# Gate and up for four column pairs: product 2 of the two halves of positions made jointly

## The chip, the cores and the metric

One core of a Trainium2 chip runs the whole program in one launch. The metric is the device time in microseconds (us) of one execution; the kernel before took 790.61 us as the median of three runs (789.64 to 792.07). TensorE (PE) multiplies 128x128 tiles with 128x512 tiles into PSUM, with its weight loads listed apart (PEld); VectorE (DVE) and ScalarE (ACT) do the elementwise work; SyncE (SP) issues the loads and GpSimd (POOL) the stores.

## The reference

For x of 2048 positions and 512 features, and F = 1792 hidden columns:

```python
def reference(A_x, A_dft_seq_re, A_dft_seq_im, A_dft_hid_re, A_dft_hid_im, B_x, B_W_gate, B_W_up, B_W_down, gate_w):
    # A: real part of a Fourier transform along features, then positions
    a = einsum("bsd,ed->bse", x, dft_hid_re);  b = einsum("bsd,ed->bse", x, dft_hid_im)
    y = einsum("ts,bse->bte", dft_seq_re, a) - einsum("ts,bse->bte", dft_seq_im, b)
    # B: a gated linear unit with a rectified gate
    h = where(gate > 0, gate, 0) * up            # gate = x @ W_gate, up = x @ W_up
    z = einsum("bsf,fd->bsd", h, W_down)
    # mixed per position
    x = A_x; g = sigmoid((x * gate_w).sum(-1, keepdims=True))
    return g * y + (1 - g) * z
```

(A and B are two inner functions in the reference; B also runs on A_x.)

## The kernel before

**Arithmetic.** Every matrix product in float32 is made of three fp32r matmuls: a value is split in a high part (an ACT cast) and a low part (a DVE subtraction), and PARTS (line 366) names the three pairs, `((1, 0), (0, 1), (0, 0))`, low with high, high with low, high with high. On top of that, products are made in blocks of 2 by 2 by 2 with seven products in place of eight (Winograd's form of Strassen's scheme), whose left and right operands are sums of blocks:

```python
LEFT = {1: ("11",), 2: ("12",), 3: ("12", 6, -1), 4: ("22",), 5: ("21", "22", 1), 6: (5, "11", -1), 7: ("11", "21", -1)}
RIGHT = {1: ("11",), 2: ("21",), 3: ("22",), 4: (6, "21", -1), 5: ("12", "11", -1), 6: ("22", 5, -1), 7: ("22", "12", -1)}
ORDER = (1, 5, 6, 2, 7, 3, 4)
BANK = {1: "x", 2: "x", 5: "m", 3: "m", 6: "y", 7: "y", 4: "t"}
```

PSUM's eight banks are four pairs x, m, y, t (PAIRS). A product accumulates on what its bank holds; a copy by ACT moves a partial result from one bank to the next (product 1 from x to y, product 7 from y to t, negated), and sums kept in SBUF (s5, s6) are added by DVE.

**Gate and up.** A Block(q, w) (lines 493-553) makes gate and up of one column pair c (0 to 6: 128 columns of gate and up in each of two parts of F) for one half q of the positions (two blocks of 512). It runs the seven products in ORDER, 12 matmuls each, 84 in all, each followed by evac (ACT copies, DVE sums u, the rectified product h). Then h_out stores h and four sums of it (hs) to hd in DRAM, the seven right operands for the product with W_down. Weights and w_prep (404-468) load and split the weights of one pair: wr raw, wah and wal high and low of the first factors, ws sums, wb0h, wb0l, wb1h, wb1l their parts, wd.

**Order of the work.** Plan (129-275) records every operation with a key in units of one matmul. PE's order is that of the code; DVE's and ACT's operations are sorted by due times worked out from the keys, SP's loads and POOL's stores by key. 51 units of SBUF are reused in turn, so an early load also has to wait for a free one. In the program's order:

1. Start (962-1020): pairs 0 and 1 together for q = 0, while inputs arrive, in ORDER_S (1, 2, 5, 6, 3, 7, 4); the first block takes products 1 and 2 with high times high first and the low part of the weights (wal) last (line 1009).
2. Pairs 2 to 6, q = 0 and q = 1 each. x of the second half is prepared by x_prep 27 units apart.
3. The transform along features (Spectral, SpectralBlock 596-663), 4 blocks.
4. Tail blocks (1067): pairs 1 and 0 for q = 1.
5. Down(0) and Down(1) (782): h times W_down; its right operands hr are loaded from hd by SP, cast by ACT (ch), subtracted by DVE (cl).
6. The transform along positions: Sequence, Joint(0) (843-932), two Sequences, Joint(1), Last. A Joint makes one product of two halves by the seven products; its right operands jc are the DFT matrix's blocks and sums of them (td). HI, LO = 31, 24 are the units by which the cast jch and the subtraction jcl are ahead of their matmuls, and the raw tile is read 90 ahead (897).

joint_sums (934-940) makes the sums for td: 16 loads (jt), 16 DVE sums and 16 stores of 512 KB, keyed 380 + 160n (1023), that is between 77 and 218 us.

Every operation is recorded through one helper, so that line 126 stands at all rows of the profile; tiles are told apart by name.

Of the kernel before, what the change touches and what calls it, by code (L numbers as in the profile page):

```python
# [14 lines left out]
P = 128  # L15
N = 512
# [262 lines left out]
def kernel(ctx: ExitStack, tc, xP, xG, wgu, wd, cr, ci, wri, gw, out):  # L279
# [94 lines left out]
    def x_load(q, b, ks=slice(0, 2), at=None):  # L374
        k, j = int(b[0]) - 1, int(b[1]) - 1
        (at or load)(piece[q, b][:, ks], xP[2 * q + j, k, :, ks])
# [6 lines left out]
    def x_sum(q, m):  # L383
        if len(RIGHT[m]) > 1:
            a, b = ((piece[q, n] if isinstance(n, str) else X[q, n][2]).all for n in RIGHT[m][:2])
            combine(X[q, m][2].all, a, b, RIGHT[m][2])
# [7 lines left out]
    def x_prep(q, m, key):  # L394
        x_raw(q, m)
        op(key, x_sum, q, m)
        op(key + 7, hi_of, X[q, m])
        op(key + 12, lo_of, X[q, m])
# [75 lines left out]
    def h_out(q, c, h, key):  # L474
        f = [buf(f"hs{n}") for n in range(2)]

        def first():
            e = E()
            e.vector.tensor_add(f[0][:, 0], h[0][:, 0], h[0][:, 1])
            e.vector.tensor_add(f[0][:, 1], h[0][:, 1], h[1][:, 1])  # L480

        def second():
            e = E()
            e.vector.tensor_add(f[1][:, 0], f[0][:, 0], h[1][:, 1])
            e.vector.tensor_add(f[1][:, 1], f[1][:, 0], h[1][:, 0])

        op(key, first)
        op(key + 6, second)
        op(key + 2, lambda: store(hd[q, 0, :, c], h[0][:, 0]))
        for n, t, k in ((1, h[1], 3), (3, f[0], 8), (5, f[1], 14)):  # L490
            op(key + k, lambda n=n, t=t: store(hd[q, n:n + 2, :, c].rearrange("x p n -> p x n"), t.all))

    class Block:


        def __init__(self, q, w, banks=PAIRS):
            self.q, self.w, self.banks = q, w, banks
            self.g = {r: buf("g" + r, (N,)) for r in ("11", "21")}
            self.s = {m: buf(f"s{m}") for m in (5, 6)}
            self.u = {r: buf("u" + r) for r in ("12", "22")}  # L500
            self.h = [buf(f"h{d}") for d in range(2)]
# [8 lines left out]
        def done(self, key):  # L510
            h_out(self.q, self.w.c, self.h, key)
# [6 lines left out]
        def one(self, m, i, k, n, first=0):  # L518
            w, x, ps = self.w.of(m, i, k), X[self.q, m], self.banks[BANK[m]]
            a, b = PARTS[n]  # L520
            mm(ps[i], w[a], x[b][:, k], start=m in FIRST and k == 0 and n == first,
               stop=m in (2, 3, 4, 7) and k == 1 and n == 2 - first)

        def evac(self, m, key):
# [11 lines left out]
            def added(r, ps, s):  # L536
                u, h = self.u[r], self.h[int(r[0]) - 1][:, 1]
                op(key, lambda: e.vector.tensor_add(u.all, ps.all, s.all))
                op(key + 1, lambda: e.vector.scalar_tensor_tensor(h, u[:, 0], 0.0, u[:, 1], op0=OP.max, op1=OP.mult))
# [10 lines left out]
            elif m == 3:  # L550
                added("12", p, self.s[6])
            elif m == 4:
                rectified("21", 0, t, -1.0)

# [59 lines left out]
    class SpectralBlock:  # L614
        def __init__(self, sp, q, ih):
            self.sp, self.q, self.ih = sp, q, ih
            self.s = {m: buf(f"s{m}") for m in (5, 6)}
# [8 lines left out]
        def product(self, m, i):  # L626
            x, w, ps = X[self.q, m], self.sp.w[m], PAIRS[BANK[m]]
# [215 lines left out]
    class Joint:  # L843


        HI, LO = 31, 24
# [40 lines left out]
        def right(self, x, hh, key):  # L887
# [9 lines left out]
            op(key - 90, read)  # L897
# [64 lines left out]
    def x_half(m, k, hi=None):  # L962
        h, l, raw = (t[:, k] for t in X[0, m])
# [8 lines left out]
    for k in halves:  # L972
        op(-99, x_load, 0, "11", k)
        op(-99, ws[0].load, 0, halves[0], k)
    op(-99, ws[1].load, 0, halves[0])
    op(-99, x_load, 0, "21")
    for w in ws:
        op(-99, w.load, 0, halves[1])
    op(-98, x_load, 0, "12")
    for w in ws:  # L980
        op(-98, w.load, 1)
    op(-98, x_load, 0, "22")
    op(-98, lambda: load(gwt[:], gw))
    for k in halves:
        op(-90, x_half, 1, k, plan.vector.tensor_copy)
        op(-90, w_half, ws[0], halves[0], k)
    op(-90, w_half, ws[1], halves[0])
    op(-90, x_half, 2, halves[0])
    op(-90, w_half, ws[0], halves[1])
    op(-90, x_half, 2, halves[1])  # L990
    op(-90, w_half, ws[1], halves[1])
    for n, m in enumerate((5, 6, 3, 7, 4)):
        key = 24 * n + 20
        for f, *a in ((x_sum, 0, m), (hi_of, X[0, m]), (lo_of, X[0, m])):
# [12 lines left out]
    for m in ORDER_S:  # L1007
        for b in start:
            if m in (1, 2) and b is start[0]:
# [8 lines left out]
    for b in start:  # L1018
        b.done(plan.now + 100)
# [3 lines left out]
    for n in range(4):  # L1023
        joint_sums(n // 2, n % 2, 380 + 160 * n)

    sequence = [(2, 0), (2, 1)]
    sequence += [(c, q) for c in range(3, NP) for q in range(2)]
    tail = [(1, 1), (0, 1)]
    spectral = Spectral()

    def blocks(sequence):
        nonlocal w
        for c, q in sequence:
            if w.c != c:
                w = Weights(c)
                if c == 1:
                    w.fetch(plan.now - 140)
                else:
                    w_prep(w, plan.now, 66 if c else 180)
            if c == 2 and q == 0:  # L1040
                for b in ("22", "11", "12", "21"):
                    x_piece(1, b)
                    op(plan.now - 100, x_load, 1, b)
                for n, m in enumerate(ORDER):
                    x_prep(1, m, plan.now - 46 + 27 * n)
            Block(q, w).run()

    blocks(sequence)
# [14 lines left out]

    lefts = [spectrum(f) for f in range(2)]
    for ih in range(2):
        SpectralBlock(spectral, 1, ih)
    blocks(tail)
# [85 lines left out]
```

## Time and profile before

| what | value |
|---|---|
| median of 3 runs | 790.61 us (789.64 to 792.07) |
| the profiled execution | 789.88 us |
| its span (first to last instruction) | 788.1 us |
| granted clock of TensorE, mean | 0.999 |
| ACT's casts of hr for Down, 128x1024 | 42 of 1.049 us |
| DMA moved | 193.84 MB, mean 246 GB/s |

The span is what the trace shows; 1.78 us of the profiled execution lie around it. Rows have the start in us, the duration, the engine, the line, the operation, out<-in, the shapes and a count xN; a bracket at the end is the idle time of that engine just before and what ended it. PE's durations are of one matmul in its pipeline and overlap: the distance of two starts is what a matmul costs in a row of them.

### The profile page before, as it was taken

How to read it: one execution, taken by the hardware profiler on the slowest of the kernel's cores; microseconds unless marked ns; L12 is line 12 of the kernel's file. 1: busy time of each engine (PE TensorE's matmuls, PEld its weight loads, DVE VectorE, ACT ScalarE, POOL GpSimd, SP SyncE). 2: the span in 40 equal slices, each digit the busy share in tenths (PEclk: the TensorE clock that was granted, in tenths of full speed). 3: DMA queues.
4: the chain of work that ended last, by engine and by line, in shares of the span. 5: the costliest groups of instructions: out<-in, count | busy, mean ns of one | idle time of the engine just before them, and what ended most of it. 6: DMA issues, size and time to landing. Idle time of an engine off the chain costs nothing.

```text
span 788.1 us, 9404 instructions
## 1 busy us (share of the span) xinstructions
PE 780.7 (99%) x3435; PEld 644.7 (82%) x3435; DVE 620.4 (79%) x663; ACT 390.4 (50%) x436; POOL 96.1 (12%) x142
## 2 busy tenths in 40 slices
PE   9999999999999999999999999999999999999997
PEld 7888888888888888888888888888888888888885
DVE  7999676667688314978764899967999999989963
ACT  6664333333354335476545464545757365574540
POOL 0011221212122111110000000200020001000200
PEclk9999999999999999999999999999999999999999
DMA  8354775576867975477688798859999889799914
GB/s 324 128 202 166 290 291 214 218 262 242 282 225 233 364 314 184 131 257 293 191 267 315 279 306 311 196 184 294 355 328 270 252 255 188 197 351 330 240 30 81
DMA packets 56574, 193.84 MB, mean 246 GB/s; under 512 B 6608, under 2 KB 6864, under 8 KB 56528
## 3 DMA queue, kind: packets, MB, share of 16 engines
q1 hardware_dynamic: 37552, 124.55, 45.2%
q0 software_dynamic: 18976, 68.69, 29.6%
q8 instruction: 27, 0.44, 0.2%
q14 instruction: 19, 0.16, 0.1%
HBM read 123.99 MB, written 60.83 MB: 235 GB/s over the span
## 4 chain that ended last, share of the span: by engine, by line
PE 97%; ACT 1%; issue 1%; DMA 1%; DVE 0%; SPq 0%; DVEq 0%
PE ps L126 97%; ACT jch L126 1%; DMA wr<-wgu 1%; SPq L126 0%; DVE v L126 0%; DVE z L126 0%; ACT js L126 0%; DVE wal L126 0%; ACT wah L126 0%; ACT ps L126 0%; DVEq L126 0%
## 5 line engine op out<-in xcount | busy, mean ns | idle before, releaser
L126 PE MATMUL ps<-ch,ll 128*128 128x512 f32 x580 | 225.6, 389 | 0.0
L126 PE MATMUL ps<-cl,lh 128*128 128x512 f32 x580 | 225.6, 389 | 0.0
L126 PE MATMUL ps<-ch,lh 128*128 128x512 f32 x580 | 225.6, 389 | 0.0
L126 ACT CAST ch<-r 128x1024 fp32r<-128x1024 f32 x96 | 97.4, 1052 | 72.5 <-DVE r L126 59.9
L126 PEld LDWEIGHTS ps<-ch,lh 128*128 128x128 f32 x580 | 108.9, 188 | 22.7
L126 PEld LDWEIGHTS ps<-ch,ll 128*128 128x128 f32 x580 | 108.9, 188 | 22.7
L126 PEld LDWEIGHTS ps<-cl,lh 128*128 128x128 f32 x580 | 108.9, 188 | 22.4
L126 DVE TENSOR_TENSOR cl<-r,ch 128x1024 fp32r<-128x1024 f32 x96 | 114.6, 1222 | 1.2 <-ACT ch L126 0.6
L126 ACT ACTIVATE ps<-ps 128x1024 f32<-128x1024 f32 (+1 forms) x34 | 32.6, 958 | 87.5 <-PE ps L126 41.0
L126 DVE TENSOR_TENSOR cl<-hr,ch 128x1024 fp32r<-128x1024 f32 (+1 forms) x56 | 59.3, 1088 | 20.4 <-ACT ch L126 18.6
L126 ACT COPY s<-ps 128x1024 f32<-128x1024 f32 x44 | 44.6, 1014 | 52.8 <-PE ps L126 52.8
L126 ACT CAST ch<-hr 128x1024 fp32r<-128x1024 f32 (+1 forms) x56 | 51.3, 942 | 26.7 <-PE ps L126 20.1
L126 DVE TENSOR_TENSOR r<-r,r 128x1024 f32<-128x1024 f32 x48 | 57.2, 1221 | 0.0
L126 POOL DMA_DIRECT2D out<-z x23 | 17.1, 743 | 322.5 <-DVE z L126 322.5
L126 DVE TENSOR_TENSOR u<-ps,s 128x1024 f32<-128x1024 f32 x28 | 34.2, 1221 | 12.4 <-PE ps L126 6.9
L126 PE MATMUL ps<-xh,wb0l 128*128 128x512 f32 x112 | 43.8, 391 | 0.0
L126 PE MATMUL ps<-xl,wb0h 128*128 128x512 f32 x112 | 43.6, 389 | 0.0
L126 PE MATMUL ps<-xh,wb0h 128*128 128x512 f32 x112 | 43.6, 389 | 0.0
L126 PE MATMUL ps<-xh,wb1h 128*128 128x512 f32 x112 | 43.6, 389 | 0.0
L126 PE MATMUL ps<-vh,xh 128*128 128x512 f32 x112 | 43.6, 389 | 0.0
L126 PE MATMUL ps<-vh,xl 128*128 128x512 f32 x112 | 43.6, 389 | 0.0
L126 PE MATMUL ps<-xh,wb1l 128*128 128x512 f32 x112 | 43.6, 389 | 0.0
(126 smaller groups left out, 1311.2 us busy)
## 6 DMA issues: line engine op xcount, KB each, us to landing
hr<-hd SPq DMA_DIRECT2D x42, 512.0 KB, 4.5
r<-cr SPq DMA_DIRECT2D x32, 512.0 KB, 5.7
r<-ci SPq DMA_DIRECT2D x32, 512.0 KB, 5.8
hd<-hs POOLq DMA_DIRECT2D x28, 512.0 KB, 5.2
out<-z POOLq DMA_DIRECT2D x23, 512.0 KB, 6.4
td<-jt POOLq DMA_DIRECT2D x16, 512.0 KB, 3.9
ad<-a POOLq DMA_DIRECT2D x16, 512.0 KB, 3.9
l<-ad SPq DMA_DIRECT2D x16, 512.0 KB, 7.2
```

The lines of the kernel that those rows point to most:

```text
L126: getattr(getattr(nc, self.engine), self.name)(*map(ap, self.a), **{k: ap(x) for k, x in self.k.items()})
```

## The change

Product 2 has the left block 12 and the right block 21, and its result goes to the output block 11 alone. For one column pair it is a product of 2 (gate, up) x 2 (blocks of 128 features) by 2 (features) x 2 (halves of positions), 8 products of one tile each, 24 matmuls for both halves. For pairs 3 to 6 the change makes it by the same seven-product scheme, 7 x 3 = 21 matmuls.

- **JointX** prepares the seven right operands jx1 to jx7 once, from the "21" pieces of x of both halves. **JointW** makes per pair four sums of weight parts of 128 columns (jws, on DVE), their high parts (jw, a cast on ACT) and low parts (DVE). Its products write bank x, one of its two banks as Y and the other as M; partial results are kept in jv and jo.
- **Joined** is a Block without product 2. With q = 0 it runs 5, 1, (joint 5, 1), 6, (joint 6), first half of 3, (joint 3, 7), 7, second half of 3, (joint 2, 4), 4; with q = 1 it runs 1, 5, 6, first half of 3, 7, second half of 3, 4. The block 11 of the output is then the sum of product 1 and jo, and a relu and product as for the others. Product 7's copy to t is made in two operations of 512.
- **Start:** both first blocks, not only the first, take products 1 and 2 with wal last. Their h is stored without the sums; **h_late** reads it again during the spectral blocks and makes the sums then.
- x's pieces "21" are loaded again ahead of the spectral blocks and split again, which frees their units in between; x_prep of the second half is 24 units apart.
- joint_sums has keys 1300 + 120n (about 295 to 393 us). Joint's HI, LO are 26, 20, and its read is 82 ahead. The two tail blocks are written out.

Over the program this makes 96 matmuls of product 2 fewer and 84 new ones.

What moves is seen in the engines' orders. The names are tiles with the number of the recording. First DVE at the boundary from pair 2 to pair 3; u are the sums of products 7 and 3 of the last block of pair 2, h its rectified results, ws and wb0l the weights of pair 3. Before:

```order
L126 TENSOR_TENSOR h_693<-g_675,ps 128x512
L126 TENSOR_TENSOR ws_700<-wr_619,wr_631 128x512
L126 TENSOR_TENSOR wb0l<-ws_685,wb0h 128x1024
L126 TENSOR_TENSOR u_713<-ps,s_636 128x1024
L126 TENSOR_TENSOR ws_700<-wr_619,ws_685 128x512
L126 TENSOR_TENSOR u_723<-ps,s_659 128x1024
```

And with the change:

```order
L126 TENSOR_TENSOR wb0l<-ws_677,wb0h 128x1024
L126 TENSOR_TENSOR jws<-wr_626 128x128
L126 TENSOR_TENSOR u_710<-ps,s_648 128x1024
L126 TENSOR_TENSOR jws<-jws,wr_626 128x128
L126 TENSOR_TENSOR jws<-wr_626 128x128
L126 TENSOR_TENSOR jws<-wr_626,jws 128x128
L126 TENSOR_TENSOR h_723<-g_681,ps 128x512
L126 TENSOR_TENSOR ws_730<-wr_626,wr_641 128x512
L126 TENSOR_TENSOR jw<-jws,jw 128x512
L126 TENSOR_TENSOR u_741<-ps,s_665 128x1024
```

Between the two sums u stood one subtraction for weights; now there stand six operations, and wb0l stands ahead of the first.

Second, ACT in the second half (q = 1) of pair 3. The first row copies product 1 from bank x to y, the two s are products 5 and 6, g is the gate of block 11, ACTIVATE ps is product 7's copy; wah, wb0h and jw belong to pair 4. Before:

```order
L126 COPY ps<-ps 128x1024
L126 COPY s_923<-ps 128x1024
L126 COPY s_941<-ps 128x1024
L126 ACTIVATE g_949<-ps 128x512
L126 CAST wah<-wr_909 128x1024
L126 ACTIVATE ps<-ps 128x1024
L126 CAST wb0h<-ws_975 128x1024
```

And with the change:

```order
L126 COPY ps<-ps 128x1024
L126 COPY s_957<-ps 128x1024
L126 CAST wah<-wr_921 128x1024
L126 CAST jw<-jws 128x512
L126 COPY s_983<-ps 128x1024
L126 CAST wb0h<-ws_973 128x1024
L126 ACTIVATE ps<-ps 128x512 x2
L126 CAST wb1h<-ws_1006 128x1024
```

The casts of wah and jw now stand ahead of the copy of product 6, and the cast of wb0h between that copy and product 7's.

Third, ACT in Joint(0); jch are the casts of the right operands, js the copies of products 5 and 6, ACTIVATE ps product 1's copy. Before:

```order
L126 CAST jch<-jc 128x1024
L126 CAST jlh<-js_4058 128x1024
L126 CAST jch<-jc 128x1024 x5
L126 ACTIVATE ps<-ps 128x512
L126 CAST jch<-jc 128x1024 x4
L126 COPY js<-ps 128x512 x2
L126 CAST jwh<-jr 128x1024
```

And with the change:

```order
L126 CAST jlh<-js_4184 128x1024
L126 CAST jlh<-js_4200 128x1024
L126 CAST jch<-jc 128x1024 x5
L126 ACTIVATE ps<-ps 128x512
L126 CAST jch<-jc 128x1024 x4
L126 COPY js<-ps 128x512
L126 CAST jch<-jc 128x1024
L126 COPY js<-ps 128x512
L126 CAST jwh<-jr 128x1024
```

The first copy js comes after nine casts jch instead of ten, and one cast stands between the two copies.

The diff, cut to its core:

```diff
+    def h_late(q, c, key):
+        h = [buf(f"hk{d}") for d in range(2)]
+        for i, n in enumerate((0, 3)):
+            op(key - 20 + i, lambda i=i, n=n: load(h[0][:, i], hd[q, n, :, c]))
+        op(key - 18, lambda: load(h[1].all, h_forms(q, c, 1)))
+        h_sums(q, c, h, key)
...
+    class Joined(Block):
+        def run(self, joint=None):
+            slots = {(1, 1): (5, 1), (6, 1): (6,), (3, 0): (3, 7), (3, 1): (2, 4)}
+            for m, i in (*((m, i) for m in ((1, 5) if self.q else (5, 1)) for i in range(2)), (6, 0), (6, 1), (3, 0), (7, 0), (7, 1), (3, 1), (4, 0), (4, 1)):
+                pe(6, self.product, m, i)
+                if i:
+                    self.evac(m, plan.now)
+                for y in slots.get((m, i), ()) if joint else ():
+                    joint.step(y)
+        def done(self, key, joint):
+            self.added("11", self.s[1] if self.q == 0 else self.banks["x"], joint.o[self.q], plan.now)
+            super().done(key)
...
+    class JointW:
+        def __init__(self, w, x, key):
...
+            op(key - 30, lambda: combine(raw[:, 0], s[:, 1, 0, 1], s[:, 1, 1, 1], 1))
+            op(key - 30, lambda: combine(raw[:, 2], s[:, 1, 0, 0], s[:, 1, 0, 1], -1))
+            op(key - 29, lambda: combine(raw[:, 1], raw[:, 0], s[:, 1, 0, 0], -1))
+            op(key - 28, lambda: combine(raw[:, 3], s[:, 1, 1, 0], raw[:, 1], -1))
+            op(key - 24, lambda: E().scalar.copy(self.t[:, 0], raw.all))
+            op(key - 20, lambda: E().vector.tensor_sub(self.t[:, 1], raw.all, f32(self.t[:, 0])))
+        def step(self, y):
+            pe(3, self.product, y)
+            self.evac(y, plan.now)
...
-        HI, LO = 31, 24
+        HI, LO = 26, 20
...
-            op(key - 90, read)
+            op(key - 82, read)
...
-            if m in (1, 2) and b is start[0]:
+            if m in (1, 2):
...
-        b.done(plan.now + 100)
+        b.done(plan.now + 8, False)
...
-        joint_sums(n // 2, n % 2, 380 + 160 * n)
+        joint_sums(n // 2, n % 2, 1300 + 120 * n)
...
-                    x_prep(1, m, plan.now - 46 + 27 * n)
+                x_prep(1, m, plan.now - 46 + 24 * n)
+            jx = JointX(plan.now + 70)
...
+            pair = [Joined(q, w) for q in range(2)]
+            joint = JointW(w, jx, plan.now)
+            for q, b in enumerate(pair):
+                b.run(None if q else joint)
+                b.done(plan.now + 8, joint)
+    for q in range(2):
+        x_piece(q, "21")
+        op(plan.now - 150 + 60 * q, x_load(q, "21"))
+        x_prep(q, 2, plan.now - 100 + 100 * q)
...
+    for c in range(2):
+        h_late(0, c, plan.now + 30 * c)
```

159 lines of the change are left out of this document (112 added, 47 removed).

## The prediction

> **What bounds the kernel now.** I read three views of the profile of before, in this order: the page's shares, the waits of PE, and the chain of waits.
>
> ```profile
> PE 780.7 (99%) x3435; PEld 644.7 (82%) x3435; DVE 620.4 (79%) x663; ACT 390.4 (50%) x436; POOL 96.1 (12%) x142
> PE 97%; ACT 1%; issue 1%; DMA 1%; DVE 0%; SPq 0%; DVEq 0%
> ```
>
> The first line gives the busy time of each engine, the second the engines' shares of the chain that ended last. PE is busy for 99% of the span and is 97% of that chain, so the end of the program is the end of a row of matmuls. A matmul less shortens it by that matmul, and nothing else shortens it except a wait of PE. Those are few (columns: us in total, times, longest):
>
> ```profile
> PE ps L126 <- DVE warm L126: 1.2, 1, 1.2
> PE ps L126 <- ACT js L126: 0.5, 2, 0.3
> PE ps L126 <- DVE wal L126: 0.4, 1, 0.4
> ```
>
> The first belongs to the warm-up, which the change leaves. The other two, 0.9 us together, are in places that it does touch.
>
> ```profile
> 8.16 542.15 PE ps L126 x2387
> ```
>
> This is a link of the chain: start, length, number. From 8.16 us on PE runs 2387 matmuls with no wait long enough to break the link, 542.15 / 2387 = 0.227 us each.
>
> The profiled execution took 789.88 us, of which 788.1 are the span and 1.78 lie around it; the median of the runs is 790.61. I make the sum as a difference and take it from both.
>
> **The matmuls.** Per column pair from 3 to 6, product 2 takes 2 halves x 12 = 24 matmuls now and 7 x 3 = 21 then. Over four pairs that is 12 fewer, and the new ones have the same shape (128x128 by 128x512).
>
> ```profile
> 67.28 0.39 PE L126 MATMUL ps<-xh,wb0l 128*128 128x512 f32 x1
> 70.00 0.39 PE L126 MATMUL ps<-xh,wb0l 128*128 128x512 f32 x1
> ```
>
> These two rows stand 12 matmuls apart in a stretch without waits: 70.00 - 67.28 = 2.72 us, the value of 12. (The 0.39 is one matmul's length in the pipeline, not its spacing.) Term one: **-2.72 us**.
>
> **The start.** Both first blocks now take their products 1 and 2 with the high parts first and wal, the low part of the weights, last.
>
> ```profile
> 6.76 0.62 ACT L126 CAST wah<-wr 128x512 fp32r<-128x512 f32 x1 [0.70 <-DMA wr<-wgu]
> 7.14 0.61 PE L126 MATMUL ps<-xh,wal 128*128 128x512 f32 x2
> 7.42 0.69 DVE L126 TENSOR_TENSOR wal<-wr,wah 128x512 fp32r<-128x512 f32 x1 [0.62 <-ACT wah L126]
> 8.16 0.50 PE L126 MATMUL ps<-xh,wal 128*128 128x512 f32 x1 [0.41 <-DVE wal L126]
> 11.02 1.29 DVE L126 TENSOR_TENSOR wal<-wr,wah 128x512 fp32r<-128x512 f32 x2
> 11.95 0.40 PE L126 MATMUL ps<-xh,wal 128*128 128x512 f32 x1
> 16.66 0.47 PE L126 MATMUL ps<-xh,wb0l 128*128 128x512 f32 x1
> 19.51 0.50 PE L126 MATMUL ps<-xh,wb0l 128*128 128x512 f32 x1
> ```
>
> The second block's first matmul came at 8.16; behind the two at 7.14 it could have come at 7.14 + 2 x 0.227 = 7.59, so 0.57 us are lost to wal, which ends at 7.42 + 0.69 = 8.11. In the new order the first four matmuls need only wah, there from 6.76 + 0.62 = 7.38, and wal at the fifth, at 7.59 + 4 x 0.227 = 8.50, after 8.11. So the 0.57 goes. What is late next is DVE: the next wal, the first of the pair at 11.02, ends at 11.71, was used at 11.95 and would now be wanted at 11.38; its order up to there is unchanged, so some 0.37 are given back and 0.2 stay. The rows at 16.66 and 19.51 are 0.1 longer than the usual 0.39: two short waits for wb0l. Ahead of that tile DVE's new order has one sum of weights less (0.6 us), which covers the 0.2, so both go: 0.2 + 0.1 + 0.1, I take **-0.45**. Ends: 0 (all is given back) and -0.8 (0.57 and the two waits).
>
> **The joint product of the DFT.** Casts and subtractions of jch and jcl come five and four matmuls nearer to their use (31, 24 to 26, 20).
>
> ```profile
> 551.81 3.88 ACT L126 CAST jch<-jc 128x1024 fp32r<-128x1024 f32 x4
> 555.58 0.39 PE L126 MATMUL ps<-jch,jlh 128*128 128x512 f32 x1
> 555.59 1.05 ACT L126 COPY js<-ps 128x512 f32<-128x512 f32 x2
> 556.21 0.50 PE L126 MATMUL ps<-jch,jll 128*128 128x512 f32 x1 [0.25 <-ACT js L126]
> 556.55 0.40 PE L126 MATMUL ps<-jcl,jlh 128*128 128x512 f32 x1
> ```
>
> ACT makes four casts in a row and only then copies the banks that PE needs. PE's spacing is 0.63 and 0.34 instead of 0.227 twice: 0.40 + 0.11 = 0.51 us, at each of the two Joints. In the changed order the first copy stands one cast (about 1 us) earlier and the second behind one cast more; the first wait goes whole, some of the second may stay. For both Joints **-0.8**; ends 0 and -1.0.
>
> **A new wait ahead of pair 3.** The first joined block starts with product 5 instead of 1. Product 5 writes bank m, which the block before frees with its last sum (u, of product 3); it is needed 12 matmuls earlier than before, and DVE has four new subtractions of 128 columns (jws) ahead of it.
>
> ```profile
> 44.16 0.39 PE L126 MATMUL ps<-xh,wal 128*128 128x512 f32 x1
> 77.16 1.00 ACT L126 ACTIVATE ps<-ps 128x1024 f32<-128x1024 f32 x1
> 78.43 1.22 DVE L126 TENSOR_TENSOR u<-ps,s 128x1024 f32<-128x1024 f32 x1
> 79.56 0.68 DVE L126 TENSOR_TENSOR ws<-wr,ws 128x512 f32<-128x512 f32 x1
> 80.16 1.22 DVE L126 TENSOR_TENSOR u<-ps,s 128x1024 f32<-128x1024 f32 x1
> L126 DVE TENSOR_TENSOR wal<-wr,wah 128x256 fp32r<-128x256 f32 x2 | 0.8, 422 | 0.0
> L126 DVE TENSOR_TENSOR hs<-hs,h 128x512 f32<-128x512 f32 x28 | 19.1, 689 | 0.3
> ```
>
> PE reaches pair 3 at 44.16 + 168 x 0.227 = 82.25. On DVE the first u waits for ACT's copy of product 7 (the row at 77.16, which can start 0.1 sooner): from about 78.05, its pitch is 79.56 - 78.43 = 1.13, three ops of 512 columns follow at 80.16 - 79.56 = 0.60, the second u takes 1.22. The width of 128 is in no row: 422 ns at 256 and 689 at 512 give 1.04 ns a column, so an estimate of 0.29 us, 0.2 in pitch. The sum is 78.05 + 1.13 + 3 x 0.2 + 3 x 0.60 + 1.22 = 82.80, and some 0.1 until PE sees it: **+0.7** on PE. What is queued behind that u on DVE (its relu, then the low parts of pair 3) has 12 matmuls to spare. Ends: 0 (the first u ready earlier) and 1.5 (DVE begins at 78.43 and takes the jws at full length).
>
> **ACT in the pairs.** In a joined second half only six matmuls of product 3 stand between 6 and 7, which share bank y, where the old order had 12; in the first half the same holds between 1 and 6.
>
> ```profile
> 68.42 0.39 PE L126 MATMUL ps<-xh,wb0h 128*128 128x512 f32 x1
> 68.84 1.01 ACT L126 COPY s<-ps 128x1024 f32<-128x1024 f32 x1 [0.62 <-PE ps L126]
> 246.97 1.23 DVE L126 TENSOR_TENSOR vl<-v,vh 128x1024 fp32r<-128x1024 f32 x1 [1.73 <-DMA hd<-h]
> ```
>
> An ACT that is idle begins its copy 68.84 - 68.42 = 0.42 after the last matmul began, and takes 1.01; with 0.05 until PE restarts that is 1.48 against 7 x 0.227 = 1.59 until the next write. So the eight places fit by 0.1 us each as long as ACT is free. In the second half it is so narrowly: between the ends of products 5 and 6 lie 2.72 us, and ACT has product 5's copy, the cast of wah (1.05, as the cast ch further below) and that of jw (0.62, as the row at 6.76) to do, 2.68. The other new place is the row at 246.97: DVE's tile for the spectral products had 1.7 us of waiting to give, and new sums come ahead of it. I take **+0.2** for both; ends 0 and 2.0.
>
> **What is covered.** The preparation of jx and jw, the later sums for h, and the shift of the sums for the DFT (16 loads and 16 stores of 512 KB from 77-218 us to some 295-393 us) are on DVE, ACT, SP and POOL. DVE is busy 79% and ACT 50% of the span, and PE hides them except at the places above; the queues are a rival below.
>
> **The sum**: -2.72 - 0.45 - 0.8 + 0.7 + 0.2 = -3.07. Of the profiled execution that makes 789.88 - 3.07 = 786.8, of the median 790.61 - 3.07 = **787.5 us**. About 0.3%, 2.4 us, is what a measurement of this kernel can tell from no change, so faster means below 788.2.
>
> **The rivals.**
>
> *ACT is late in each second half.* If the cast of jw only begins when product 6 ends, its 0.62 less the margin of 0.1 are left on PE, 0.5 at four places, +2.0: **789.5**. For it speaks how full ACT is there; against it that the casts are due early and that ACT is half idle else.
>
> *The waits stay.* Where DVE sets the pace, an earlier PE only waits elsewhere: the start gives 0, the Joints 0, the boundary costs 1.5, ACT 0.2, and 790.61 - 2.72 + 1.7 = **789.6**. For it speaks the short wait at 16.66; against it that the waits view names none of PE's after 8.16 but js.
>
> *A matmul is worth less than its spacing.* If half of the spacing were left behind by each, the 12 would bring 1.36, and the time would be **788.9**; 2387 matmuls at 0.227 speak against it. The Trainium skill (TensorE: Matmul & The Clock Gate, section Back-to-back issue gap) gives a sustained spacing of about 131 ns for 512 columns; by that figure term one would be an estimated 1.57 us. The trace's 227 ns differs, and the measurement decides.
>
> *Slower: Down's loads come late.* The moved loads and stores meet the reloads of h for Down.
>
> ```profile
> 295.00:366.00 71.00, 71.00 (x314) 58.72 (x313) 55.39 (x61) 40.89 (x47) 8.28 (x12) 1.00 0.64 223
> 546.00:565.00 19.00, 18.75 (x83) 15.19 (x83) 18.64 (x18) 16.77 (x20) 0.84 (x1) 1.00 1.02 350
> 321.89 27.74 SPq L126 DMA_DIRECT2D hr<-hd  x11
> 348.86 0.39 PE L126 MATMUL ps<-xh,wd 128*128 128x512 f32 x1
> hr<-hd SPq DMA_DIRECT2D x42, 512.0 KB, 4.5
> td<-jt POOLq DMA_DIRECT2D x16, 512.0 KB, 3.9
> L126 DVE TENSOR_TENSOR cl<-hr,ch 128x1024 fp32r<-128x1024 f32 x42 | 51.0, 1222 | 19.4 <-ACT ch L126 17.6 <-PE ps L126 1.2 <-issue 0.3
> L126 ACT CAST ch<-hr 128x1024 fp32r<-128x1024 f32 x42 | 43.7, 1049 | 19.5 <-PE ps L126 13.5 <-DMA hr<-hd 4.7 <-DVE cl L126 1.3
> SPq L126 <- DVE cl L126: 55.8, 26, 8.8
> ```
>
> The last two numbers of a window are the DMA share and GB/s. From 295 to 366 the engines moved 223 GB/s, at full share (546 to 565) 350. The 32 transfers are 16.8 MB over 98 us, 171 GB/s more: 394, or 44 too many, which leaves 3.1 MB, 9 us of work, standing at 366; as the windows are uneven I take 12. The first hr is issued at 321.89 and Down starts after 348.86: 27 us, less 4.5 to land, 1.05 to cast and 1.22 to subtract leaves 20.2. The price begins there. SP stands up to 8.8 us for a free buffer; if it stands so at two of the new loads ahead of hr, the delay is 12 + 17.6 = 29.6, and 9.4 us reach PE: **796.9**. Against it: one such stand alone (20.8) is just absorbed. In a sentence by itself, the Trainium skill (DMA: Bandwidth & Descriptors, section Issuing engines are not separate DMA queues) says that transfers run on the same 16 engines whichever engine issued them, so that SP's loads and POOL's stores would not evade each other.
>
> **How the numbers follow.** Forecast 0.59, late ACT 0.15, waits stay 0.15, matmuls worth less 0.02, slower 0.09. The low end takes the better bounds: 790.61 - 2.72 - 0.8 - 1.0 = 786.1, so 786.0. The high end is the dearest of the rivals that are not slower, 789.6, and 0.8 for the spread of the medians: 790.4. Only the late loads lie outside. Below 788.2 are the forecast's cases unless two of its losses are larger, 0.58; above 793.0 the late loads, 0.09; the rest is 0.33.
>
> **What would show it.** Right: 12 matmuls fewer, no wait for wal at 8 us, at most one short wait for js at each Joint, and one wait of PE for a u of 0.5 to 1 us at 82 us. Wrong: waits of PE for ACT's s at the sixth matmuls of the pairs; a wait for ch or cl soon after 346 us, with a DMA share near 1 ahead of it (late loads); or PE reaching 234 us no earlier than before (the pairs give back what they save).

## The result, and the profile after

The changed kernel took 788.81 us, the median of 10 runs (787.85 to 790.92), against 790.39 us for ten runs of the kernel before. The ratio is 0.998, with a 95% interval of 0.9972 to 0.9988: 1.6 us less, between 0.9 and 2.2. The forecast was 787.5, with a range of 786.0 to 790.4. The profiled execution took 789.17 us, with a span of 787.3; that is 0.7 less than the profiled one of before.

The page of the changed kernel, busy time and chain:

```profile
PE 778.7 (99%) x3423; PEld 641.5 (81%) x3423; DVE 652.6 (83%) x716; ACT 403.2 (51%) x465; POOL 96.9 (12%) x144
PE 92%; issue 2%; DVE 2%; DMA 1%; ACT 1%; POOL 0%; SPq 0%; DVEq 0%; ACTq 0%; POOLq 0%
```

There are twelve matmuls less and 2.0 us less of busy PE, but PE's share of the chain has fallen from 97% to 92%: the chain now leaves PE in places where it did not before. PE's waits, in the same columns as before:

```profile
PE ps L126 <- DVE warm L126: 1.2, 1, 1.2
PE ps L126 <- DVE vl L126: 1.1, 1, 1.1
PE ps L126 <- ACT wah L126: 0.5, 1, 0.5
PE ps L126 <- DVE u L126: 0.5, 1, 0.5
```

The waits for wal and js are gone from the list, and three others stand in it. A wait in this list is only the part in which PE was idle; what it costs is the distance of two starts less the usual 0.227 us. Added up over the starts of all matmuls that gives, for the two profiled executions:

| place | before | after | difference | forecast |
|---|---|---|---|---|
| 12 matmuls | | | -2.72 | -2.72 |
| start: pair 2 begins at | 44.16 | 44.07 | -0.1 | -0.45 |
| boundary to pair 3 | 0 | 0.73 | +0.7 | +0.7 |
| second halves of pairs 3 to 6 | 0 | 0.28 | +0.3 | +0.2, with the next |
| features' transform, 248 us | 0 | 1.35 | +1.35 | |
| two Joints | 1.03 | 0.66 | -0.4 | -0.8 |
| sum | | | -0.8 | -3.1 |

The sum is that of the two spans, 787.3 - 788.1 = -0.8; what the table leaves out (small spacings between these places, the time behind the last matmul) is about 0.1 each and cancels. So the table says where the expected time went, in these two executions. The medians differ by 1.6 and not by 0.8; which of the places is cheaper in the other executions wasn't recorded. PE reached the features' transform at 233.07 us, 1.65 earlier than before (234.72): the pairs give back the two rows of 0.7 and 0.3 and keep the rest. Four places in rows, first the start:

```profile
7.69 0.62 ACT L126 CAST wah<-wr 128x512 fp32r<-128x512 f32 x1 [1.54 <-DMA wr<-wgu]
8.36 0.51 PE L126 MATMUL ps<-xh,wah 128*128 128x512 f32 x1 [0.51 <-ACT wah L126]
```

ACT waits for the load of weights wr, which landed 0.93 us later than before (7.69 against 6.76); PE waits for the high part instead of the low one. Then the boundary to pair 3:

```profile
77.95 1.23 DVE L126 TENSOR_TENSOR u<-ps,s 128x1024 f32<-128x1024 f32 x1 [1.05 <-ACT ps L126]
79.49 0.28 DVE L126 TENSOR_TENSOR jws<-wr,jws 128x128 f32<-128x128 f32 x1
81.50 1.22 DVE L126 TENSOR_TENSOR u<-ps,s 128x1024 f32<-128x1024 f32 x1
82.77 0.50 PE L126 MATMUL ps<-xh,wb0l 128*128 128x512 f32 x1 [0.46 <-DVE u L126]
```

The first u begins at 77.95, six operations follow, the second u ends at 82.72 and PE starts 0.05 later. The 128-column subtraction took 0.28. Third, the features' transform, on POOL, DVE and PE:

```profile
237.10 0.72 POOL L126 DMA_DIRECT2D hd<-h  x1 [15.22 <-DVE h L126]
238.84 0.55 POOL L126 DMA_DIRECT2D hd<-h  x1 [1.02 <-DVE h L126]
hd<-h POOLq DMA_DIRECT2D x1, 512.0 KB, 6.7
hd<-h POOLq DMA_DIRECT2D x1, 256.0 KB, 5.6
241.12 1.22 DVE L126 TENSOR_TENSOR xl<-x,xh 128x1024 fp32r<-128x1024 f32 x1
243.88 1.23 DVE L126 TENSOR_TENSOR vs<-v,vs 128x1024 f32<-128x1024 f32 x1 [1.54 <-DMA hd<-h]
246.86 1.22 DVE L126 TENSOR_TENSOR vl<-vs,vh 128x1024 fp32r<-128x1024 f32 x1
248.14 0.50 PE L126 MATMUL ps<-vl,xh 128*128 128x512 f32 x1 [1.08 <-DVE vl L126]
```

The third and fourth row give the size of the two stores above them and the time until they landed. h_out stores block 11 in one transfer of 256 KB and the blocks 21 and 22 in one of 512 KB, so the first store is that of 21 and 22, and it landed at 237.10 + 6.7 = 243.8. The sum vs, for the left operand of product 3, waits 1.54 us for just this landing. It reads nothing of h: it needs a unit of SBUF that h still holds. Three of the gate's reductions and vl come behind it, and PE stands. In the kernel before the same two operations, and the same two stores, read:

```profile
227.81 0.58 POOL L126 DMA_DIRECT2D hd<-h  x1 [4.98 <-DVE h L126]
239.13 1.22 DVE L126 TENSOR_TENSOR vs<-v,vs 128x1024 f32<-128x1024 f32 x1
239.52 0.71 POOL L126 DMA_DIRECT2D hd<-h  x1 [11.13 <-DVE h L126]
241.47 1.23 DVE L126 TENSOR_TENSOR vl<-vs,vh 128x1024 fp32r<-128x1024 f32 x1
```

There vs waited for nothing, and vl was ready almost 6 us before its use. Block 11 was stored at 227.81, now at 238.84, 11 us later. The blocks 21 and 22 were stored at 239.52, 2.4 us later than now, and the tile that waited for that landing was the last vl (the row at 246.97 in the prediction), which was ready at 248.20, 3 us before its use. Last, Joint(0) on ACT and PE:

```profile
551.28 3.91 ACT L126 CAST jch<-jc 128x1024 fp32r<-128x1024 f32 x4
555.09 0.57 ACT L126 COPY js<-ps 128x512 f32<-128x512 f32 x1
555.57 1.04 ACT L126 CAST jch<-jc 128x1024 fp32r<-128x1024 f32 x1
555.71 0.50 PE L126 MATMUL ps<-jch,jll 128*128 128x512 f32 x1
556.05 0.39 PE L126 MATMUL ps<-jcl,jlh 128*128 128x512 f32 x1
```

PE, which arrives about 0.3 earlier than before, still starts when the first copy ends: its spacing there is 0.45 and 0.34 instead of 0.63 and 0.34. As before, four casts stand in a row right ahead of that copy; they begin 0.53 earlier (551.28 against 551.81).

### The profile page after: what moved, and what is told of

Read it like the earlier page. It is cut to its first block, busy times and chain, and to the rows that moved or that the text cites. A ratio compares the mean times of both kernels' runs of the same rounds, so it can differ in the third digit from the quotient of the medians.

```text
span 787.3 us, 9523 instructions
## 1 busy us (share of the span) xinstructions
PE 778.7 (99%) x3423; PEld 641.5 (81%) x3423; DVE 652.6 (83%) x716; ACT 403.2 (51%) x465; POOL 96.9 (12%) x144
## 4 chain that ended last, share of the span: by engine, by line
PE 92%; issue 2%; DVE 2%; DMA 1%; ACT 1%; POOL 0%; SPq 0%; DVEq 0%; ACTq 0%; POOLq 0%
PE ps L126 92%; DMA hd<-h 1%; DVE u L126 1%; DMA wr<-wgu 1%; POOL hd L126 0%; DVE h L126 0%; DVE gx L126 0%; ACT jch L126 0%; SPq L126 0%; DVE v L126 0%; DVE z L126 0%; DVE vl L126 0%; ACT ps L126 0%; ACT js L126 0%; ACT wah L126 0%
## 5 line engine op out<-in xcount | busy, mean ns | idle before, releaser
L126 ACT COPY s<-ps 128x1024 f32<-128x1024 f32 x48 | 48.7, 1014 | 68.1 <-PE ps L126 64.1
L126 PE MATMUL ps<-vl,xh 128*128 128x512 f32 x112 | 43.7, 390 | 1.1 <-DVE vl L126 1.1
L126 PE MATMUL ps<-xl,wb1h 128*128 128x512 f32 x112 | 43.6, 389 | 0.0
```

The lines of the kernel that those rows point to most:

```text
L126: getattr(getattr(nc, self.engine), self.name)(*map(ap, self.a), **{k: ap(x) for k, x in self.k.items()})
```

## The experiments

Each kernel was timed beside the kernel before; the ratios are to that one, with 95% intervals of 0.0008 to 0.0017 to each side. The changed kernel's own ratio is 0.998. Every edit is made to the changed kernel.

**1. The gate's reductions later.** Do they make the wait for vl?

```diff
-        gate(t, plan.now + 30 + 50 * t)
+        gate(t, plan.now + 90 + 50 * t)
```

> The changed kernel, with the gate's reductions (gx on DVE) keyed 60 units (13.6 us) later, so that none stands ahead of the low parts vl for the third product of the features' transform. Theory: PE's wait of 1.24 us for vl at 248 us, with 0.11 behind it, is made by three gx operations of 0.61 us pitch behind a sum that itself waited 1.54 us for a store of h to land; without them vl ends near 246.2, before PE wants it at 246.9, the wait goes whole and nothing else is late next: 1.3 us less than the changed kernel, 787.5 us, 0.9963 of the kernel before. Rival: the landing of the store sets the time, gx only fills it, and the next vl or the sums a come late instead: no gain, 788.8, with a wait of about 1 us under another name between 246 and 260 us.

It took 789.21 us, ratio 0.9986 (0.9978 to 0.9995). The wait for vl was gone, but the time was not less. The move gave the units of SBUF and DVE another order later on, and in the Sequence PE waited for cl:

```profile
495.94 0.50 PE L126 MATMUL ps<-cl,lh 128*128 128x512 f32 x1 [0.48 <-DVE cl L126]
```

With what follows that is 0.75, and at 227 us another 0.37. Pair 2 also began 0.5 later in that execution (44.59). And vs began at 235.40 without a wait for a unit, so the run doesn't tell the reductions from the unit. It shows that the wait can be taken away, not what it is worth.

**2. jws and jw later.** All six operations of JointW on weights get keys 20 higher:

```diff
-            op(key - 30, lambda: combine(raw[:, 0], s[:, 1, 0, 1], s[:, 1, 1, 1], 1))
+            op(key + 20 - 30, lambda: combine(raw[:, 0], s[:, 1, 0, 1], s[:, 1, 1, 1], 1))
```

> The changed kernel, with the preparation of the four weight sums (jws and jw) keyed 20 units (4.5 us) later, so that on DVE only two subtractions of weights stand between the two sums u at the boundary to pair 3. Theory: the wait for u at 82.8 us (0.62 and 0.11) is DVE's queue, and the second u ends near 81.6 before PE arrives at 82.1: that wait goes, and so do the four of 0.07 at the casts of jw ahead of product 6's copy in the second halves: 0.7 to 1.0 less than the changed kernel, 787.9 us. Rival: the wait moves to the low part wb1l or to jw, which are now behind the u, within the first joined block: 0.3 less at most, 788.5.

It took 788.36 us, ratio 0.9976 (0.9967 to 0.9984): less than the changed kernel, but inside both intervals. In the trace PE runs over the boundary without a stop:

```profile
82.28 0.39 PE L126 MATMUL ps<-xh,wd 128*128 128x512 f32 x1
82.51 0.39 PE L126 MATMUL ps<-xh,wb0l 128*128 128x512 f32 x1
```

The 0.73 were DVE's queue, as forecast. The small waits of the second halves stayed at 0.06 to 0.07 each, although no cast of jw stands ahead of product 6's copy any more, so these don't come from it; that part of the expectation was wrong. This execution also shows the wait at 248 us in a dearer form, in the last section.

**3. No joint product.** Pairs 3 to 6 made by plain blocks:

```diff
-            pair = [Joined(q, w) for q in range(2)]
-            joint = JointW(w, jx, plan.now)
-            for q, b in enumerate(pair):
-                b.run(None if q else joint)
-                b.done(plan.now + 8, joint)
+            for q in range(2):
+                Block(q, w).run()
```

> The changed kernel, with pairs 3 to 6 made by plain blocks (product 2 for each half, 12 matmuls more over the program; no jx, jw) and everything else as changed. Theory: 12 matmuls cost their spacing, 2.72 us, and the waits that came with the joint products (0.73 for u at the boundary, 0.28 at the copies of product 6) go: 1.7 above the changed kernel, 790.5 us. If the wait for vl belongs to the end of the last joined pair it goes too: 789.2. Rival: a matmul is worth half its spacing here: 0.35 above the changed kernel, 789.2, with the spacing between neighbouring matmuls of product 2 below 0.2 us in the trace.

It took 790.0 us, ratio 0.9996 (0.9987 to 1.0004). PE had no wait at the boundary, none in the second halves and none for vl (0.1 at 251 us; 0.33 at 270 us is new), so by the trace it is the second of the two cases expected, though the median lies 0.8 above its value. The profiled execution fits it: 789.17 + 2.72 - 0.73 - 0.28 - 1.35 = 789.5, and it took 789.58. So the waits of the table that are new in the changed kernel come with the joint product, and what else the change does is worth about nothing beside the Joints' 0.4. Between neighbours of product 2 the spacing is 0.227.

**4. The old order at the start.**

```diff
-            if m in (1, 2):
+            if m in (1, 2) and b is start[0]:
```

> The changed kernel, with the old order of the second first block (products 1 and 2 with the low part of the weights first), all else as changed. Theory: the profile of the changed kernel showed no gain at the start only because its load of weights landed 0.9 us later in that execution; for the same landing the old order waits 0.6 us longer, of which DVE's row gives some back: 0.4 us above the changed kernel, 789.2. Rival: after 11 us DVE sets the pace of the start whatever PE's order is, and nothing is lost: 788.8.

It took 788.80 us, ratio 0.9985 (0.9976 to 0.9994): that of the changed kernel. In its profiled execution the load came late and the old order did wait longer:

```profile
9.29 0.50 PE L126 MATMUL ps<-xh,wal 128*128 128x512 f32 x1 [1.53 <-DVE wal L126]
```

Pair 2 began at 44.78 us here. In the eight traces with the new order and as late a load (landing at 7.5 to 8.0) it began between 44.07 and 44.59, so with a late load the new order was 0.2 to 0.7 earlier than this one execution of the old. With an early load (6.4 to 6.9) it began between 43.97 and 44.43, in experiments 2, 3 and 7, and before, with the old order, at 44.16. There the new order only moves the wait: PE had none at 8 us and stood at 11 us for the next wah, here in experiment 7:

```profile
11.17 0.73 PE L126 MATMUL ps<-xh,wah 128*128 128x512 f32 x2 [0.60 <-ACT wah L126]
```

In the twelfth trace, of experiment 6, it began at 46.05: the first loads landed 1 us later, and the clock came to its full speed only at 9.45 us, in the others by 7.3. In the median the new order is worth nothing that can be seen.

**5. The features' operands nearer together.** This puts vs ahead of the sums of h and vl ahead of the gate, and leaves the later order as it is.

```diff
-        spectral.prep(m, plan.now - 44 + 16 * n if n < 3 else plan.now - 30 + 12 * n)
+        spectral.prep(m, plan.now - 44 + 16 * n if n < 3 else plan.now - 30 + 10 * n)
```

> The changed kernel, with the operands of the features' transform prepared 10 units apart from product 2 on and not 12, so that on DVE the sum vs for product 3 stands ahead of the four sums of h, and its low part vl ahead of the gate's reductions; the gate's keys stay. Theory: PE's wait for vl at 248 us (1.35 with what follows, and more in runs where the store of h lands later or the clock sinks behind it) is that place in DVE's queue; it goes, and nothing later is reordered: 1.3 less than the changed kernel, 787.5 us, with less spread between the runs. The kernel with the gate moved lost the same wait and gained nothing in the median because its later order made a wait of 0.75 for cl at 496 us and one at 227. Rival: the wait for vl is in few runs only, so that the median does not move: 788.6 to 788.9; or vs itself now holds DVE up until the store lands: a wait of PE for vl or xl of about 1 us as before, 788.8.

It took 789.87 us, ratio 0.9996 (0.9987 to 1.0004), slower than the changed kernel. vs was done at 238.3, but another tile now stood for the unit of h, ACT's copy of product 6:

```profile
244.90 1.01 ACT L126 COPY s<-ps 128x1024 f32<-128x1024 f32 x1 [1.16 <-DMA hd<-h]
245.97 0.50 PE L126 MATMUL ps<-vh,xl 128*128 128x512 f32 x1 [1.53 <-ACT s L126]
```

This ended the theory that the place in DVE's queue makes the wait. The store that s waited for is that of block 11, issued at 239.17 and landed at 244.8, not the one that vs waits for in the changed kernel. Whoever takes a unit of h waits until its store has landed.

**6. Three edits at once**: experiments 2 and 5, and HI, LO = 24, 18.

> The changed kernel with three edits: the features' operands 10 units apart, jws and jw 20 units later, and HI, LO of the Joints 24, 18 (first copy js after eight casts). Theory: the waits add up, 1.35 for vl, 0.73 for u and 0.28 in the second halves, 0.66 at the Joints: 3.0 less than the changed kernel, 785.8 us, 0.994 of the kernel before. Rival: DVE and ACT are full at these places and the waits come back under other names, half of it at most: 787.3.

It took 788.75 us, ratio 0.9988 (0.998 to 0.9997). No wait was left at the boundary or at the Joints, but ACT's s cost 2.04 us at 247, as in 5. The profiled execution was the slowest of the twelve (791.94), so how much of the 2.9 that the median lacks is due to s isn't shown.

**7. The sums for the DFT back in the pairs.**

```diff
-        joint_sums(n // 2, n % 2, 1300 + 120 * n)
+        joint_sums(n // 2, n % 2, 380 + 160 * n)
```

> The changed kernel, with the sums for td back at their old keys (16 loads, sums and stores between 77 and 218 us and not 295 to 393). Theory: where they are PE never waits for them, neither here nor there; the reloads hr have 20 us in hand and lose 3.5 us in landing; the time is that of the changed kernel within 0.5: 788.8. Rival one (late loads): the moved transfers cost PE something in Down, and undoing them gains 0.5 or more: 788.3 or less. Rival two: with the joint products DVE has no room for 16 sums of 1.22 us in the pairs, and PE waits there for u, jo or wb0l: 789.5 or more.

It took 792.63 us, ratio 1.0027 (1.0017 to 1.0037): 3.8 above the changed kernel. The number falls under rival two, but the path that it named isn't there: no wait for u or jo was added in the pairs; in the profiled execution (791.05 us) the loss stands at the features' transform:

```profile
245.05 0.50 PE L126 MATMUL ps<-vh,xl 128*128 128x512 f32 x1 [0.67 <-ACT s L126]
250.13 0.50 PE L126 MATMUL ps<-vl,xh 128*128 128x512 f32 x1 [1.83 <-DVE vl L126]
```

That is 3.05 us with what follows, against 1.35. So moving the sums away belongs to the change: without it more than its gain is lost. The rest of the median's loss isn't in this execution, and its place stays open.

**8. The Joints as before.** HI, LO = 31, 24 and the read at 90.

> The changed kernel, with HI, LO of the Joints and the read back at 31, 24 and 90. Theory: the wait for js at each Joint is 0.51 again and not 0.33, 0.37 for both: 789.2 us, and the rows at 555 and 705 us are as in the kernel before. Rival: the wait at the Joints is set by what PE brings with it, not by the place of the copy, and stays at 0.33: 788.8.

It took 788.87 us, ratio 0.9983 (0.9975 to 0.9992); 0.4 us can't be told in the median. In the trace the rows of before are back, 0.64 and 0.34 between starts at both Joints, 0.37 more in all:

```profile
555.71 0.50 PE L126 MATMUL ps<-jch,jll 128*128 128x512 f32 x1 [0.26 <-ACT js L126]
556.05 0.40 PE L126 MATMUL ps<-jcl,jlh 128*128 128x512 f32 x1
```

**9. Block 11 of a second half summed early.**

```diff
                 if i:
                     self.evac(m, plan.now)
+                    if m == 1 and self.q:
+                        self.added("11", self.banks["x"], self.jo, plan.now)
...
-            self.added("11", self.s[1] if self.q == 0 else self.banks["x"], joint.o[self.q], plan.now)
+            if not self.q:
+                self.added("11", self.s[1], joint.o[0], plan.now)
...
             for q, b in enumerate(pair):
+                b.jo = joint.o[q]
                 b.run(None if q else joint)
```

> The changed kernel, with the output block 11 of a joined second half (q = 1) summed right after product 1 and not after product 4, so that it is no longer the last of the block's results and its store to hd is issued some 9 us earlier; all later orders on DVE stay. Theory: the tile that PE waits for at 246 to 250 us (vl, or ACT's s in the kernel with the features' operands nearer) has to take a unit of SBUF from h, which is free only when h's store has landed, at 243.9; the change made that store the last of the block. With the sum early PE has no wait over 0.2 us there: 1.3 less than the changed kernel, 787.5 us, and less spread. Rival: the unit comes free with the other part of h (21 and 22), whose store is as late as before: the wait stays at 0.8 to 1.7, 788.8.

It took 788.93 us, ratio 0.9978 (0.9969 to 0.9987), the changed kernel's within the intervals; the runs lay between 788.34 and 789.38, a spread of 1.0 against 3.1. vs no longer waited and the wait for vl was gone, but the next tile in want of a unit waited for the store of the sums hs:

```profile
246.27 1.23 DVE L126 TENSOR_TENSOR vl<-v,vh 128x1024 fp32r<-128x1024 f32 x1 [0.94 <-DMA hd<-hs]
250.94 0.50 PE L126 MATMUL ps<-vh,xl 128*128 128x512 f32 x1 [0.69 <-ACT ps L126]
```

It reaches PE as 0.95 us through DVE's sums and ACT's copy, and at 227 us PE lost 0.31 where it lost 0.07 before. So the late sum of block 11 did cause the wait of vs, but not by the path that was expected. Block 11 was stored at 225.63, 13 us earlier; the store of 21 and 22, for which vs had waited, was issued at 237.24 and landed at 243.4, about when it does in the changed kernel, but vs began at 240.52, before that landing: it got another unit. Units are so short there that a later tile then waited for the next store, and the rival's number came.

**10. Early sum, late jws, and HI, LO = 24, 18 together.**

> The kernel with the early sum of block 11, and jws and jw 20 units later, and HI, LO of the Joints 24, 18. Theory: 1.35 for vl, 0.73 for u, 0.2 in the second halves and 0.66 at the Joints go: 2.9 less than the changed kernel, 785.9 us, 0.994 of the kernel before. Rival: the start, which is ruled by the landing of the first loads, and one place that is late next keep a third of it: 786.9.

It took 787.28 us (786.63 to 787.52), ratio 0.9958 (0.9945 to 0.997): by medians and by ratios faster than the kernel before by 3.1 and 3.3 us, and than the changed kernel by 1.5 and 1.7 (with the intervals, between 0.6 and 2.9). PE's waits:

```profile
PE ps L126 <- DVE warm L126: 1.2, 1, 1.2
```

Only the warm-up is left in the list; shorter than the list shows are 0.31 at 226 us and 0.06 at three places. The expected 785.9 was 1.4 too low; the 0.95 of experiment 9 wasn't in its profiled execution (span 784.9, 786.63 us), which was the fastest of its runs.

**11. The sums for the DFT in half the time.**

```diff
-        joint_sums(n // 2, n % 2, 1300 + 120 * n)
+        joint_sums(n // 2, n % 2, 1360 + 60 * n)
```

> The changed kernel, with the sums for td made in less time: 16 loads, sums and stores keyed 1360 + 60n and not 1300 + 120n, so that they share the time with the first reloads hr for Down. Theory of the prediction: DMA carries no more than 350 GB/s, the loads hr come late by the backlog, and PE waits for ch or cl between 346 and 400 us by 3 us or more: 792 us or above. Rival: the changed kernel's windows show 401 to 416 GB/s at 335 to 395 us, so there is room left, SP issues hr in time, and PE does not wait there: 788.8 within 0.4.

It took 797.82 us, ratio 1.009 (1.0073 to 1.0107). This is the rival of late loads. ACT waits for hr, and PE for ACT and DVE:

```profile
370.06 1.04 ACT L126 CAST ch<-hr 128x1024 fp32r<-128x1024 f32 x1 [5.54 <-DMA hr<-hd]
371.16 0.50 PE L126 MATMUL ps<-ch,ll 128*128 128x512 f32 x1 [1.42 <-ACT ch L126]
372.42 0.50 PE L126 MATMUL ps<-cl,lh 128*128 128x512 f32 x1 [0.76 <-DVE cl L126]
```

From 371 to 397 us PE lost 7.8 us. A load hr took up to 18.9 us to land, in the changed kernel up to 13.9 and before up to 8.4. So the mechanism exists; the changed kernel's spacing of 120 units stays clear of it, as no wait for ch or cl stands in its list.

**12. No joint product, and HI, LO = 24, 18**: the counterpart of 10.

> The changed kernel with pairs 3 to 6 made by plain blocks (12 matmuls more, no jx, jw) and HI, LO of the Joints 24, 18: what is left of the waits of the kernel with the early sum (787.28 us) on both sides of the joint product. Theory: the 12 matmuls cost their spacing of 2.72, less the 0.3 to 0.5 that the joint pairs still wait at their copies: 787.28 + 2.3 = 789.6 us, with PE waiting nowhere over 0.3 us after 12 us. Rival: a matmul is worth half its spacing: 787.28 + 1.36 - 0.4 = 788.2 us.

It took 789.35 us, ratio 0.9989 (0.998 to 0.9998), with no wait of PE but the warm-up's in the list (0.33 at 270 us is below what it shows). Against experiment 10 that is 0.9989 - 0.9958 = 0.0031 of 790.4, or 2.4 us, with the intervals between 1.2 and 3.7. The profiled spans say the same, 787.3 - 784.9 = 2.4: on ground without the other waits the twelve matmuls bring their 2.72 less about 0.3, which is what PE's small waits differ by. Against experiment 3, which differs by HI, LO alone, it is 0.0007 or 0.6 us, inside the intervals, and in the traces the 0.68 that the Joints cost there and not here.

## Why the prediction was right, and where it was off

The direction and the range held; half of the forecast gain came. The range is a weak test: its upper end is 790.4, which is what the kernel before itself measured over ten runs. The 788.81 is also above the 788.2 below which the prediction called the result faster, in the case that it gave a chance of 0.33. And the number is nearest to that of a rival that is wrong, the matmul worth half its spacing with 788.9: there it is coincidence, as the rows below show. Step by step:

- **The matmuls: right.** The term of 2.72 for 12 matmuls agrees with the balance of the two traces and with the 2.4 us between experiments 12 and 10. The rival of a matmul worth half its spacing is out: it gave 1.36 - 0.4 there, and would leave 1.36 of the balance without a place.
- **The boundary: right.** 0.73 measured against 0.7, by the path that was named; experiment 2 takes it away by DVE's order alone.
- **The start: wrong.** The step took the landing of one execution's load as given. It lay between 6.4 and 8.0 us in fourteen traces. With a late one the new order waits for wah where the old one waited for wal, and with an early one it waits at 11 us instead, where the step gave back 0.37 of 0.57 and 0.4 to 0.9 were lost. Median gain: none that experiment 4 could see, where 0.45 were forecast.
- **The Joints: half.** PE does wait for that copy, but the step took it to come one cast, about 1 us, earlier, and 0.37 came for 0.8. Nine casts stand ahead of it and not ten, but the four in a row between product 1's copy and js, on which the step rests, stayed four. So the copy came only 0.5 us earlier, and as PE came 0.3 earlier too, 0.2 of the wait went. The prediction said "the first wait goes whole"; with three casts in that row (HI, LO = 24, 18, experiments 6 and 10) it does.
- **The features' transform: mis-sized, and with the wrong cause.** The prediction saw that vl's slack of 1.7 us would shrink and booked 0.2 with ACT's small waits, where 1.63 came. It looked for the cost in DVE's queue. The cost was a unit: vs was given one that held the blocks 21 and 22 of h, whose store was still on its way. That store isn't late, it is issued 2.4 us earlier than before. What is late is block 11: the joint product makes it the last result of a block, stored 11 us later. Experiment 9 shows that this is the cause (with the sum early vs gets another unit), and 5 that units stay short (another tile waits, for the store of block 11). That the late sum works by keeping its own tiles' units in use is argued, not shown.
- **ACT in the second halves: about right.** 0.07 at each of four places, not 0.5. Moving jw's cast left them, and in experiment 2 ACT stood idle ahead of product 6's copy, so no cast delays it; that the copy itself uses up the margin of 0.1 is likely, but not shown.
- **Late loads: rightly a rival, rightly kept small.** Its price was built on 350 GB/s as the most that DMA moves, and that was wrong:

```profile
335.00:355.00 20.00, 20.00 (x90) 16.57 (x89) 19.93 (x23) 13.01 (x16) 4.88 (x8) 1.00 1.01 401
355.00:375.00 20.00, 20.00 (x90) 16.57 (x89) 20.00 (x23) 11.97 (x13) 2.74 (x4) 1.00 1.03 412
375.00:395.00 20.00, 20.00 (x89) 16.54 (x89) 17.36 (x18) 11.56 (x14) 2.15 (x4) 1.00 1.03 416
```

In these windows of the changed kernel the last two numbers, DMA share and GB/s, are 1.01 to 1.03 and up to 416. (The moved transfers really lie between 305 and 407 us.) Why full engines moved 350 in one stretch and 416 in another wasn't tried. The Trainium skill (DMA: Bandwidth & Descriptors, section Where 436 GB/s comes from) gives 435 GB/s as the ceiling of the ports and about 358 for transfers between HBM and SBUF; the trace is near the first and above the second, and the measurement decides.

What stays open: in which share of the executions the wait at 248 us is long. The changed kernel's runs spread over 3.1 us, those of experiment 9 over 1.0, and profiles with the same code at that place show 0.1 (experiment 11), 1.0 (8), 1.35, 3.8 and 3.9 us (4 and 2). They go with the landing of the store of 21 and 22, which took 5.4, 6.3, 6.7, 7.5 and 7.4 us. The 1.35 of one profile is one draw of it.

## What to carry to other kernels

When an engine is busy 99% of the span, count its instructions first, but then ask of every buffer that the change keeps longer who gets its memory next: here a result that became the last of its block cost 1.35 of the 3.07 that were forecast, at a place that the diff hardly touches. Ask also which transfer ended the wait, by its issue and size: two stores of the same name stood here, and the one that was waited for wasn't the late one. A term that rests on when a load landed in one profile is worth nothing until a second profile shows the same landing. Small waits are judged better together than one by one: experiments 2 and 9 alone brought 0.4 and nothing, inside the intervals, and with the Joints' edit 1.5 to 1.7. Whether one of these waits hid another, or the spread of the runs hid the gains, isn't shown.

## What the runs showed of the hardware

After a long wait PE went on at a lower clock. Experiment 4 waited 0.42 and 1.66 us for vh and vl within 2 us, and then:

```profile
247.00:250.00 3.00, 1.35 (x5) 0.61 (x4) 3.00 (x8) 3.00 (x4) 0.08 (x1) 1.00 0.09 22
250.00:254.40 4.40, 4.40 (x13) 3.40 (x13) 3.54 (x7) 2.23 (x4) 1.35 (x2) 0.61 0.83 275
250.73:254.14 3.41, 3.41 (x9) 2.64 (x8) 2.56 (x7) 1.52 (x3) 0.72 (x1) 0.50 0.93 312
```

PE was busy 1.35 of 3 us, then the granted clock (third number from the end) was 0.61 over 4.4 us, eight matmuls stood 0.43 us apart and not 0.227, and the wait cost 1.6 us more. The third row is the stretch at half clock alone: 3.41 us. The same came in experiments 2 (0.50 and 1.66), 6 (2.04) and 11 (1.58 and 1.03), 3.41 us long each time; not after 1.35 in the changed kernel, 1.69 in 5, and 1.99 in 7.

The clock records of these four traces show when it comes. The drop begins at 250.73, 249.92, 248.38 and 373.08 us (experiments 4, 2, 6, 11), the clock's first rise to full speed was at 4.97, 4.16, 9.45 and 4.44, and between the two lie 72, 72, 70 and 108 times 3.413 us. So in these runs the clock changed only at the ends of stretches of 3.413 us that are counted from its first rise. What PE's spacings lost inside the one stretch ahead of a drop was 2.2, 2.1, 2.2 and 2.6 us; the most that was lost in a stretch without a drop behind it was 1.9 (in experiments 7, where the rest of the 1.99 fell into the next stretch, and 11). So about 2 us lost in one such stretch were followed by half clock in the next, and less wasn't. The Trainium skill (TensorE: Matmul & The Clock Gate, section Why this matters for your kernels) warns of gaps of more than about 3 us; here, by the trace, less was enough.
